# A padded identity, matmuls and one-row tables in place of DRAM round trips in a linear-attention and rational-FFN kernel

## The chip, the cores and the metric

The kernel runs on one core of a Trainium2 chip. The metric is the device time of one execution in microseconds. Three runs of the kernel before took 593.08, 595.28 and 597.16 us; their median is 595.28 us. All inputs and outputs are float32 in DRAM.

## The reference

Eight heads of size 48, a batch of 4 and 768 steps of a decayed linear attention, and then a feed-forward layer whose activation is a quotient of two polynomials:

```python
for t in range(S):
    cur = einsum('bhd,bhe->bhde', u * k[t], v[t])          # bonus of the present step
    y[t] = einsum('bhd,bhde->bhe', r[t], state + cur)
    state = w[..., None] * state + einsum('bhd,bhe->bhde', k[t], v[t])
h = x @ w_in                                               # x: y as 3072 x 384, w_in 384 x 2048
g = (a0 + a1*h + a2*h**2 + a3*h**3) / (1 + |b0|*|h| + |b1|*h**2 + 1e-6)
out = g @ w_out                                            # w_out 2048 x 384
```

The decay `w` and the bonus `u` are tables of 8 x 48 = 384 numbers.

## The kernel before

**Attention.** The 3072 tokens are 24 blocks of 128 (`blk`, L306: block n is batch n % 4). A block's k and r are scaled by powers of the decay (`scale_k`, `scale_r`), transposed on TensorE (`tk`, `tr`, L375), multiplied with each other (`a`, L398 and L399) and masked; k and v give the state's growth (`kv`, L420 and L421), and `y` (L448) joins both. The state that a block leaves is multiplied by the decay over a block, `w128` (`carry`, L459), for the block of the same batch four numbers later. The bonus of the present step is worked out beside it: `bonus_a` (L356), `bonus_b` (times the table `ub`, L361), `bonus_sum`, `bonus_v`, and `y_ev` (L453) adds it. `x` (L467) transposes the sum for the feed-forward part.

**Feed-forward.** It runs in 97 slices (L500): `f1` (L491, nine matmuls, two of them a slice but for the last two), ten element-wise operations on ScalarE and VectorE (`z`, `q`, `t`, `ln`, `ex`; `u3`, `hi`, `p`, `d`, `lo`), and `f2` (L495 to L497, six matmuls, two a slice). The weights come as 28 pieces, each loaded (`cl`, L235), split by a short chain (`c0`, L246, to `co`, L266) into two rounded parts, and kept.

**The tables.** `pro_load` to `pro_natural` make the powers of the decay. `pro_last` leaves the decay over a block as one column of 384 numbers in three columns of 128 (`wl`), `pro_wl` writes it to DRAM (`wld`, L179) and `pro_w128` reads it back with heads of 48 on partitions 0 and 64 (L183, L184). `pro_uw` reads `u` and `w` into all 128 partitions and `pro_ub` multiplies them on GpSimd (L150). `pro_squares` (L132 to L147, called `sq` below) works out constants of the quotient on VectorE. `pro_flag` (L198 to L211), `pro_flag_turn` and `pro_flag_min` test whether the inputs lie in the range of the fast formula; at the very end each engine loads the answer `okf` and branches over `general()` (L986, L987).

**What sets the order.** Every step is a task with engines, durations that the author wrote down, dependencies, buffers and a key. `run` (L783) plays them through a list scheduler: at each moment an engine takes the ready task with the lowest key whose buffers are free. The tasks are then issued in the order that came out, each engine's queue in that order. Where TensorE finds no ready task between 1.6 and 132.098 us of that play, a filler is put in its queue (L878 to L885, called warm): one matmul of 128 x 128 ones that nothing reads (L894). So a change of any task can move all others.

## Time and profile before

| what | us |
|---|---|
| median of three runs | 595.28 |
| the profiled execution: its own time | 593.54 |
| its span, first to last instruction | 591.8 |
| TensorE busy, of the span | 570.1 (96%) |
| VectorE busy | 506.0 (86%) |
| ScalarE busy | 454.6 (77%) |
| GpSimd busy | 179.7 (30%) |

The profile's page gives busy times by engine, and in the chain of waits the work that ended last at each moment. TensorE, 71% of that chain, is busy nearly all the time, but 739 of its 6194 matmuls are fillers, all of them before 138 us. The other engines do their table work, the splitting of the weights and the first half of the attention in that stretch. Later the span is the feed-forward part's two products, with the rest of the attention between them.

### The profile page before, as it was taken

How to read it: one execution, taken by the hardware profiler on the slowest of the kernel's cores; microseconds unless marked ns; L12 is line 12 of the kernel's file. 1: busy time of each engine (PE TensorE's matmuls, PEld its weight loads, DVE VectorE, ACT ScalarE, POOL GpSimd, SP SyncE). 2: the span in 40 equal slices, each digit the busy share in tenths (PEclk: the TensorE clock that was granted, in tenths of full speed). 3: DMA queues.
4: the chain of work that ended last, by engine and by line, in shares of the span. 5: the costliest groups of instructions: out<-in, count | busy, mean ns of one | idle time of the engine just before them, and what ended most of it. 6: DMA issues, size and time to landing. Idle time of an engine off the chain costs nothing.

```text
span 591.8 us, 15041 instructions
## 1 busy us (share of the span) xinstructions
PE 570.1 (96%) x6194; PEld 551.5 (93%) x6194; DVE 506.0 (86%) x791; ACT 454.6 (77%) x758; POOL 179.7 (30%) x199
## 2 busy tenths in 40 slices
PE   8969999999989999999999999999999999999996
PEld 7868998989989999999999988999999999999996
DVE  5669989899989889788899899788898897878784
ACT  8658678977968886888866857888778778778883
POOL 5677998996730000000240182000240100000000
PEclk9979999999989999999999999999999999999999
DMA  9886284964600000021221240020220000000000
GB/s 192 136 196 152 79 185 132 219 150 68 99 1 2 28 1 27 2 41 35 41 47 43 42 89 28 1 58 18 42 62 1 14 30 0 3 28 1 27 2 33
DMA packets 94269, 34.78 MB, mean 59 GB/s; under 512 B 87280, under 2 KB 90608, under 8 KB 94192
## 3 DMA queue, kind: packets, MB, share of 16 engines
q1 hardware_dynamic: 94192, 33.74, 26.4%
q8 instruction: 51, 0.84, 0.6%
q14 instruction: 26, 0.21, 0.1%
HBM read 29.01 MB, written 4.72 MB: 57 GB/s over the span
## 4 chain that ended last, share of the span: by engine, by line
PE 71%; DVE 11%; DMA 9%; ACT 5%; issue 2%; SPq 1%; POOL 0%; ACTq 0%; DVEq 0%
PE h L491 29%; PE o L495 10%; PE o L496 10%; PE o L497 10%; DMA sto<-in_moe_w_out_dram 4%; DMA sti<-in_moe_w_in_dram 3%; PE y L448 2%; PE kv L420 2%; PE a L398 1%; DMA kh<-in_k_dram 1%; DVE q L554 1%; PE warm L894 1%; ACT cp L246 1%; PE tk L375 1%; PE x L467 1%
## 5 line engine op out<-in xcount | busy, mean ns | idle before, releaser
L491 PE MATMUL h<-xthi,wi_hi 128*128 128x256 f32 x576 | 165.3, 287 | 1.9 <-DVE g L562 1.9
L491 PE MATMUL h<-xthi,wi_lo 128*128 128x256 f32 x576 | 163.2, 283 | 0.0
L491 PE MATMUL h<-xtlo,wi_hi 128*128 128x256 f32 x576 | 163.2, 283 | 0.0
L495 PE MATMUL o<-wo_hi,g 128*128 128x384 f32 x384 | 132.0, 344 | 0.0
L497 PE MATMUL o<-wo_hi,g 128*128 128x384 f32 x384 | 128.6, 335 | 0.0
L496 PE MATMUL o<-wo_lo,g 128*128 128x384 f32 x384 | 128.6, 335 | 0.0
L491 PEld LDWEIGHTS h<-xthi,wi_hi 128*128 128x128 f32 x576 | 110.0, 191 | 2.7 <-issue 2.2
L491 PEld LDWEIGHTS h<-xthi,wi_lo 128*128 128x128 f32 x576 | 110.4, 192 | 0.0
L491 PEld LDWEIGHTS h<-xtlo,wi_hi 128*128 128x128 f32 x576 | 110.3, 191 | 0.0
L522 ACT ACTIVATE q<-h 128x512 f32<-128x512 f32 (+1 forms) x97 | 57.5, 593 | 67.8 <-PE h L491 67.3
L550 DVE SCALAR_TENSOR_TENSOR g<-h,sig,z 128x512 fp32r<-128x512 f32 (+1 forms) x97 | 72.1, 744 | 38.5 <-ACT z L540 34.7
L526 ACT ACTIVATE q<-q,off,root 128x512 f32<-128x512 f32 (+1 forms) x97 | 78.4, 808 | 0.4
L531 ACT ACTIVATE t<-h,off,root 128x512 f32<-128x512 f32 (+1 forms) x97 | 74.6, 769 | 4.8 <-PE h L491 4.5
L554 DVE SCALAR_TENSOR_TENSOR q<-q,sig,g 128x512 f32<-128x512 f32 (+1 forms) x97 | 75.0, 774 | 2.5
L544 DVE SCALAR_TENSOR_TENSOR h<-t,sig,h 128x512 f32<-128x512 f32 (+1 forms) x97 | 72.1, 743 | 4.5 <-ACT q L522 2.5
L558 DVE SCALAR_TENSOR_TENSOR h<-h,sig,q 128x512 f32<-128x512 f32 (+1 forms) x97 | 72.8, 751 | 2.7
L536 ACT ACTIVATE z<-q,lnb 128x512 f32<-128x512 f32 (+1 forms) x97 | 69.9, 720 | 4.2 <-DVE g L562 2.0
L495 PEld LDWEIGHTS o<-wo_hi,g 128*128 128x128 f32 x384 | 72.4, 189 | 0.7
L496 PEld LDWEIGHTS o<-wo_lo,g 128*128 128x128 f32 x384 | 72.5, 189 | 0.0
L497 PEld LDWEIGHTS o<-wo_hi,g 128*128 128x128 f32 x384 | 72.1, 188 | 0.0
L540 ACT ACTIVATE z<-z,lnb 128x512 f32<-128x512 f32 (+1 forms) x97 | 69.7, 718 | 2.6
L562 DVE TENSOR_TENSOR g<-h,z 128x512 fp32r<-128x512 f32 (+1 forms) x97 | 65.9, 679 | 1.0
(129 smaller groups left out, 957.4 us busy)
## 6 DMA issues: line engine op xcount, KB each, us to landing
sti<-in_moe_w_in_dram SPq DMA_DIRECT2D x12, 512.0 KB, 5.6
sto<-in_moe_w_out_dram SPq DMA_DIRECT2D x16, 384.0 KB, 3.8
vn<-in_v_dram SPq DMA_DIRECT2D x24, 192.0 KB, 3.2
rh<-in_r_dram SPq DMA_DIRECT2D x24, 192.0 KB, 3.7
kh<-in_k_dram SPq DMA_DIRECT2D x24, 192.0 KB, 4.4
out_dram<-os SPq DMA_DIRECT2D x24, 192.0 KB, 1.9
vs<-in_v_dram SPq DMA_DIRECT2D x19, 96.0 KB, 4.1
ub<-in_u_dram SPq DMA_DIRECT2D x1, 192.0 KB, 4.3
```

Source lines behind the costliest of these rows:

```text
L491: nc.tensor.matmul(o, wt_[:, cc, ts(j, P)], x_[:, cc], start=(n == 0), stop=(n == 3 * NCC - 1))
L495: nc.tensor.matmul(o, hi, wo_hi[:, j], start=(j == 0), stop=False)
L496: nc.tensor.matmul(o, hi, wo_lo[:, j], start=False, stop=False)
L497: nc.tensor.matmul(o, lo, wo_hi[:, j], start=False, stop=(j == NJ - 1))
L526: nc.scalar.activation(g["q"], g["q"], AF.Square, scale=RB, bias=KB)
L531: nc.scalar.activation(g["t"], g["h"], AF.Square, scale=RA, bias=KA)
L536: nc.scalar.activation(g["z"], g["q"], AF.Ln, scale=2.0 ** -LN_SHIFT, bias=lnb[:, 2:3])
L540: nc.scalar.activation(g["z"], g["z"], AF.Exp, scale=-1.0, bias=lnb[:, 1:2])
L544: nc.vector.scalar_tensor_tensor(g["h"], g["t"], KAP, g["h"], op0=ALU.add, op1=ALU.mult)
L550: nc.vector.scalar_tensor_tensor(g["hi"], g["h"], c0, g["z"], op0=ALU.add, op1=ALU.mult)
L554: nc.vector.scalar_tensor_tensor(g["q"], g["q"], qe, g["hi"].bitcast(F32), op0=ALU.add, op1=ALU.mult)
L558: nc.vector.scalar_tensor_tensor(g["h"], g["h"], c0, g["q"], op0=ALU.add, op1=ALU.subtract)
```

## The change

The column `wl` is re-laid on TensorE: the identity is a slice of a wider zeroed tile `identw`, so that a shifted slice of it picks 48 of 128 rows and drops them at partition 0 or 64 (`pro_pairs`, ten matmuls into one PSUM tile; ScalarE copies it to `w128`). `u` and `w` are read into one partition, multiplied there, spread to all partitions by a matmul with a row of ones (`pro_spread`) and copied out by ScalarE (`pro_ub_all`, task `ube`). The range test's first part gets the key 400 and waits for slice 64 of 97.

```diff
--- before.py
+++ after.py
@@ -60,7 +60,9 @@
 
 
     wones = cst.tile([P, P], mybir.dt.bfloat16, name="wones")
-    ident = cst.tile([P, P], F32, name="ident")
+    identw = cst.tile([P, D + P + D], F32, name="identw")
+    ident = identw[:, D : D + P]
+    ones = cst.tile([1, P], F32, name="ones")
     mask = cst.tile([P, HALF], F32, name="mask")
     wraw = cst.tile([P, NCC], F32, name="wraw")
     wcol = cst.tile([P, NCC], F32, name="wcol")
@@ -73,7 +75,6 @@
     sq = cst.tile([P, NCC], F32, name="sq")
     cen = cst.tile([P, NCC], F32, name="cen")
     wl = cst.tile([P, NCC], F32, name="wl")
-    wld = dram.tile([DM], F32, name="wld")
     wrn = cst.tile([P, H, D], F32, name="wrn")
     wkn = cst.tile([P, H, D], F32, name="wkn")
     w128 = cst.tile([P, NP], F32, name="w128")
@@ -97,7 +98,9 @@
         nc.sync.dma_start(wraw, w.rearrange("h d -> (h d)").rearrange("(c p) -> p c", p=P))
         tab["zero"] = at.tile([P, P], F32, tag="m", name="zero", bufs=NM)
         nc.gpsimd.memset(tab["zero"], 0.0)
+        nc.gpsimd.memset(identw, 0.0)
         make_identity(nc, ident)
+        nc.vector.memset(ones, 1.0)
         nc.gpsimd.memset(wones, 1.0)
 
     def pro_mask():
@@ -113,9 +116,9 @@
         nc.sync.dma_start(coef[:, 4:6], b.partition_broadcast(P))
 
     def pro_uw():
-        nc.sync.dma_start(ub, u.partition_broadcast(P))
-        tab["wb"] = at.tile([P, H, D], F32, tag="m", name="wb", bufs=NM)
-        nc.sync.dma_start(tab["wb"], w.partition_broadcast(P))
+        for nm, src in (("ur", u), ("wr", w)):
+            tab[nm] = at.tile([1, H, D], F32, tag="m", name=nm, bufs=NM)
+            nc.sync.dma_start(tab[nm].rearrange("o h d -> o (h d)"), src.rearrange("h d -> (h d)").unsqueeze(0))
 
     def pro_beta():
         nc.scalar.activation(beta[:, 0:2], coef[:, 4:6], AF.Abs)
@@ -147,7 +150,15 @@
         v_.tensor_scalar(lnb[:, 2:3], QE, 2.0 ** -LN_SHIFT, None, op0=ALU.mult)
 
     def pro_ub():
-        nc.gpsimd.tensor_mul(ub, ub, tab.pop("wb"))
+        nc.gpsimd.tensor_mul(tab["ur"], tab["ur"], tab["wr"])
+
+
+    def pro_spread():
+        tab["up"] = ps_a.tile([P, 512], F32, tag="pa", name="pup")
+        nc.tensor.matmul(tab["up"][:, 0:DM], ones, tab["ur"].rearrange("o h d -> o (h d)"), start=True, stop=True)
+
+    def pro_ub_all():
+        nc.scalar.copy(ub.rearrange("p h d -> p (h d)"), tab["up"][:, 0:DM])
 
 
     def pro_clamp():
@@ -175,13 +186,20 @@
         nc.vector.tensor_mul(wl, tab["pw"][:, :, P], sq)
 
 
-    def pro_wl():
-        nc.sync.dma_start(wld.rearrange("(c p) -> p c", p=P), wl)
+    def pro_pairs():
+        p_ = tab["wp"] = ps_a.tile([P, 512], F32, tag="pa", name="pwp")
+        for h in range(H):
+            rows = slice(HALF * (h % 2), HALF * (h % 2) + D)
+            cs = range(h * D // P, (h * D + D - 1) // P + 1)
+            for c in cs:
+                x = D + h * D - c * P
+                nc.tensor.matmul(
+                    p_[rows, h // 2 : h // 2 + 1], identw[:, x : x + D], wl[:, c : c + 1], start=(c == cs[0]), stop=(c == cs[-1])
+                )
 
     def pro_w128():
-        wp = wld.rearrange("(p two d) -> two d p", two=2, d=D)
-        nc.sync.dma_start(w128[0:D, :], wp[0])
-        nc.sync.dma_start(w128[HALF : HALF + D, :], wp[1])
+        for rows in (slice(0, D), slice(HALF, HALF + D)):
+            nc.scalar.copy(w128[rows], tab["wp"][rows, 0:NP])
 
     def pro_turn(c, i):
         if c == 0:
@@ -672,7 +690,7 @@
             add(("sk", n), lambda e, n=n: scale_k(n, e), t, {"D": 0.47, "G": 0.96}, [("Lk", n), ("tab", 1)])
             add(("sr", n), lambda e, n=n: scale_r(n, e), t + 0.5, {"D": 0.47, "G": 0.96}, [("Lr", n), ("tab", 0)])
             add(("ba", n), lambda e, n=n: bonus_a(n, e), t + 2, {"G": 0.96, "D": 0.47}, [("sk", n), ("sr", n)], new=[("m", ("m", n))])
-            add(("bb", n), lambda e, n=n: bonus_b(n, e), t + 3, {"G": 0.96, "D": 0.47}, [("ba", n), ("ub",)], use=[("m", n)])
+            add(("bb", n), lambda e, n=n: bonus_b(n, e), t + 3, {"G": 0.96, "D": 0.47}, [("ba", n), ("ube",)], use=[("m", n)])
             add(("bs", n), lambda e, n=n: bonus_sum(n), t + 6, {"D": 0.47}, [("bb", n)], new=[("dt", ("dt", n))], use=[("m", n)])
             add(("bv", n), lambda e, n=n: bonus_v(n, e), t + 8, {"G": 0.96, "D": 0.47}, [("bs", n), ("Lv", n)], use=[("m", n), ("dt", n), ("v", n)])
             add(("tk", n), lambda e, n=n: trk_pe(n), t + 1, {"P": 0.44}, [("sk", n), ("id",), w_("a", n - 1)], new=[("ps", ("tk", n))])
@@ -744,6 +762,8 @@
         add(("beta",), lambda e: pro_beta(), 14, {"A": 0.8}, [("coef",)])
         add(("sq",), lambda e: pro_squares(), 16, {"D": 2.4}, [("beta",)])
         add(("ub",), lambda e: pro_ub(), 6, {"G": 0.96}, [("uw",)])
+        add(("ubp",), lambda e: pro_spread(), 6, {"P": 0.66}, [("ub",)], new=[("pa", ("up", 0))])
+        add(("ube",), lambda e: pro_ub_all(), 6, {"A": 0.37}, [("ubp",)], use=[("up", 0)])
         add(("cl_",), lambda e: pro_clamp(), -99, {"D": 0.13}, [("w",)])
         add(("ctr",), lambda e: pro_center(), -99, {"A": 0.55}, [("cl_",)])
         for c in range(NCC):
@@ -756,15 +776,15 @@
                 add(("turn", c, i), lambda e, c=c, i=i: pro_turn(c, i), -99 + c, {"P": 0.21},
                     [(("pow", "inv")[i], c), ("id",), first if c else None], new=[] if c else [("pa", new)], use=[new] if c else [])
             add(("tab", i), lambda e, i=i: pro_natural(i), -99, {"A": 0.37}, [("turn", c, i) for c in range(NCC)], use=[new])
-        add(("flag",), lambda e: pro_flag(), 200, {"D": 1.6}, [("cl_",), ("sq",)])
-        add(("flagt",), lambda e: pro_flag_turn(), 200, {"P": 0.1}, [("flag",)], new=[("ps", ("fl", 0))])
-        add(("flagm",), lambda e: pro_flag_min(), 200, {"D": 0.4}, [("flagt",)], use=[("fl", 0)])
+        add(("flag",), lambda e: pro_flag(), 400, {"D": 4.0}, [("cl_",), ("sq",), ("lo", 2 * NS // 3)])
+        add(("flagt",), lambda e: pro_flag_turn(), 400, {"P": 0.1}, [("flag",)], new=[("ps", ("fl", 0))])
+        add(("flagm",), lambda e: pro_flag_min(), 400, {"D": 0.4}, [("flagt",)], use=[("fl", 0)])
         add(("w",), lambda e: None, -99, {"S": 0.55})
         add(("wl",), lambda e: pro_last(), 10, {"D": 0.1}, [("pow", NCC - 1)])
-        add(("wld",), lambda e: pro_wl(), 10, {"S": 0.6}, [("wl",)])
-        add(("w128",), lambda e: pro_w128(), 12, {"S": 1.1}, [("wld",)])
-
-    COLS = {"turn": 256, "flagt": 256, "tk": 1024, "tr": 1024, "x": 768, "kv": 1180, "a": 1620, "y": 1736, "f1": 2304, "f2": 2304, "warm": 128}
+        add(("wp",), lambda e: pro_pairs(), 10, {"P": 0.6}, [("wl",), ("id",)], new=[("pa", ("wp", 0))])
+        add(("w128",), lambda e: pro_w128(), 12, {"A": 0.4}, [("wp",)], use=[("wp", 0)])
+
+    COLS = {"turn": 256, "flagt": 256, "tk": 1024, "tr": 1024, "x": 768, "wp": 40, "ubp": 1536, "kv": 1180, "a": 1620, "y": 1736, "f1": 2304, "f2": 2304, "warm": 128}
     TICK = 10.24 / 3
     ticks = {}
```

Because the order is worked out anew, the queues change around these steps. First SP's queue, the one that issues all transfers, at the place of the two table loads. Before (`ub`, `wb`: the two tables; `wld`, `w_94`: the round trip; `rh`, `kh`: r and k of a block; `sto`: a piece of w_out):

```order
L116 DMA ub<-in_u_dram 128x384
L118 DMA wb<-in_w_dram 128x384
L179 DMA wld<-wl 128x3x1
L322 DMA rh_113<-in_r_dram 128x8x48
L235 DMA sto_529<-in_moe_w_out_dram 128x768
L322 DMA rh_115<-in_r_dram 128x8x48
L112 DMA coef<-in_moe_a_dram 128x4
L113 DMA coef<-in_moe_b_dram 128x2
L235 DMA sto_593<-in_moe_w_out_dram 128x768
L183 DMA w_94<-wld 48x4x1
L184 DMA w_94<-wld 48x4x1
```

The same place now:

```order
L121 DMA ur<-in_u_dram 1x384
L121 DMA wr<-in_w_dram 1x384
L340 DMA rh_113<-in_r_dram 128x8x48
L340 DMA rh_115<-in_r_dram 128x8x48
L115 DMA coef<-in_moe_a_dram 128x4
L116 DMA coef<-in_moe_b_dram 128x2
L253 DMA sto_559<-in_moe_w_out_dram 128x768
L340 DMA kh_114<-in_k_dram 128x8x48
L340 DMA kh_116<-in_k_dram 128x8x48
L253 DMA sto_642<-in_moe_w_out_dram 128x768
```

The round trip's three transfers are gone, the tables are one row each, and the fifth and sixth weight pieces (`sto_559`, `sto_642`; before `sto_529`, `sto_593`) come behind both loads of `coef`, the sixth behind two loads of k as well.

Second, ScalarE's queue at the same time. Before (`cp<-sto`: the first step of splitting a piece, `c0`; `ysa<-tr`, `ysb<-tr`: the transposed r of block 3; `beta` to `root`: constants of `coef`):

```order
L246 ACTIVATE cp_595<-sto_529 128x384
L240 ACTIVATE upo_604<-sto_529 128x384
L269 COPY ysa_120<-tr_582 64x512
L269 CAST wo_hi<-bitso_565 128x384
L269 COPY ysb_121<-tr_582 64x512
L121 ACTIVATE beta<-coef 128x2
```

Now:

```order
L287 COPY ysa_120<-tr_579 64x512
L287 COPY ysb_121<-tr_579 64x512
L258 ACTIVATE upo_615<-sto_438 128x384
L287 CAST wi_hi<-bitsi_2_538 128x512
L264 ACTIVATE cp_644<-sto_559 128x384
L124 ACTIVATE beta<-coef 128x2
L125 ACTIVATE cabs<-coef 128x6
L128 ACTIVATE half<-rx 128x2
L129 ACTIVATE root<-half 128x2
L258 ACTIVATE upo_671<-sto_559 128x384
L287 CAST wo_hi<-bitso_692 128x384
L264 ACTIVATE cp_711<-sto_642 128x384
L161 COPY ub<-pup 128x384
```

The copies of block 3's transposed r, for which the product `a` of block 3 waits, now stand ahead of the fifth piece's first step, not behind it; the bonus table `ub` is written behind the first step of the sixth piece. On VectorE the fifteen operations of `sq`, which stood between the bonus of block 3 and its `y_ev`, now stand ahead of block 1's `bonus_b`, and so ahead of the whole bonus of blocks 0 and 1 and of the first `x`.

Third, VectorE and TensorE at the range test's end. Before, TensorE's transpose of the flag stood in the middle of the program:

```order
L375 MATMUL tr_4917<-ident,rh_115 128x128 x4
L375 MATMUL tr_4925<-ident,rh_111 128x128 x4
L215 MATMUL fl_4932<-ident,oks 1x128
L495 MATMUL o_0_4670<-wo_hi,g_4825 128x384
L496 MATMUL o_0_4670<-wo_lo,g_4825 128x384
```

Now it is TensorE's last instruction (`o_1_7856` is the output of the last token tile):

```order
L513 MATMUL o_1_7856<-wo_hi,g_8095 128x384
L514 MATMUL o_1_7856<-wo_lo,g_8095 128x384
L515 MATMUL o_1_7856<-wo_hi,g_8095 128x384
L233 MATMUL fl_8121<-identw,oks 1x128
L1006 TENSOR_LOAD okf
L1007 COMPARE_AND_BRANCH
```

The eleven VectorE operations of the test itself stand between `p` and `d` of slice 65; its result now passes TensorE and VectorE behind the last `f2`, and all engines load it after that.

TensorE's queue holds 896 fillers where it held 739. Ahead of the first `x` there are 295 (before 218): 44 of them between block 3's `a` and the spread of the bonus row, and 116 between the spread and that `x`, where 47 stood between `a` and `x` and 47 more ahead of `a` (25 there now). Between the first `x` and the last filler there are 601 (before 521).

## Rows read from the trace of the kernel before

**Rows 1.** Windows: length, busy PE, PEld, DVE, ACT, POOL, then TensorE clock, DMA share, GB/s.

```profile
20.00:40.00 20.00, 14.21 (x256) 13.30 (x254) 11.93 (x25) 8.84 (x21) 13.49 (x14) 0.83 0.81 125
...
60.00:80.00 20.00, 20.00 (x373) 18.97 (x368) 18.44 (x30) 13.26 (x26) 18.79 (x20) 1.00 0.31 82
...
200.00:250.00 50.00, 50.00 (x351) 49.90 (x351) 43.76 (x62) 39.03 (x60) 0.00 (x0) 1.00 0.03 12
```

**Rows 2.** Chain of waits, merged: start us, us, what; 0 to 200 us.

```profile
21.23 10.87 DMA sto<-in_moe_w_out_dram
...
40.30 0.33 PE x L467 x3
...
51.31 0.79 DVE half L134
...
173.04 2.15 PE h L491 x18
```

**Rows 3.** Windows of 2 us, columns as in rows 1.

```profile
20.00:22.00 2.00, 1.80 (x47) 1.52 (x46) 1.96 (x4) 1.96 (x5) 1.65 (x2) 1.00 0.77 218
...
24.00:26.00 2.00, 2.00 (x32) 1.92 (x29) 1.07 (x3) 1.10 (x2) 1.00 (x1) 1.00 0.92 24
```

**Rows 4.** Waits between 20 and 42 us: total, times, longest.

```profile
ACT cp L246 <- DMA sto<-in_moe_w_out_dram: 6.3, 1, 6.3
...
PE a L398 <- ACT ysa L269: 5.1, 1, 5.1
...
DVE rx L124 <- ACT cabs L122: 3.1, 1, 3.1
```

**Rows 5.** Timeline of SP's queue: start us, us, issue.

```profile
20.16 0.43 SPq L179 DMA_DIRECT2D wld<-wl  x1
...
22.28 3.46 SPq L112 DMA_DIRECT2D coef<-in_moe_a_dram  x1
```

**Rows 6.** Transfers by kind on the page: count, size, median us to landing.

```profile
sto<-in_moe_w_out_dram SPq DMA_DIRECT2D x16, 384.0 KB, 3.8
...
coef<-in_moe_a_dram SPq DMA_DIRECT2D x1, 2.0 KB, 11.5
```

**Rows 7.** Timeline of TensorE, 24 to 36.8 us.

```profile
25.40 0.61 PE L375 MATMUL tr<-ident,rh 128*128 128x128 f32 x4
25.84 2.79 PE L894 MATMUL warm<-wones 128*128 128x128 bf16 x47
```

**Rows 8.** Timeline of ScalarE, 8 to 10.3 us, with idle time before.

```profile
10.21 0.59 ACT L269 COPY ysa<-tr 64x512 f32<-64x512 f32 x1 [1.57 <-PE tr L375]
```

**Rows 9.** Timeline of TensorE, the last fillers.

```profile
136.96 0.56 PE L894 MATMUL o<-wones 128*128 128x128 bf16 x7
```

**Rows 10.** Instructions on tile half, near the end of sq: durations, first and last start.

```profile
L146 DVE TENSOR_SCALAR sig<-half x1: 147/147/147, 55.8 to 55.8; 128x1 f32<-128x1 f32 x1
```

**Rows 11.** Instructions on the range test's tile okw, columns as before.

```profile
L198 DVE TENSOR_TENSOR okw<-wraw,wcol x1: 346/346/346, 162.9 to 162.9; 128x3 f32<-128x3 f32 x1
...
L211 DVE TENSOR_REDUCE oks<-okw x1: 163/163/163, 166.5 to 166.5; 128x1 f32<-128x8 f32 x1
```

**Rows 12.** Windows of 5 to 20 us, columns as in rows 1.

```profile
160.00:170.00 10.00, 8.11 (x51) 7.82 (x50) 9.86 (x22) 7.49 (x12) 5.13 (x6) 0.91 0.18 24
```

**Rows 13.** Timeline of VectorE, lo of slice 66.

```profile
446.02 0.69 DVE L562 TENSOR_TENSOR g<-h,z 128x512 fp32r<-128x512 f32 x1
```

**Rows 14.** Timeline of TensorE, f2 of slice 66.

```profile
451.50 0.34 PE L495 MATMUL o<-wo_hi,g 128*128 128x384 f32 x1
```

**Rows 15.** Chain of waits at the end.

```profile
586.30 0.19 PE o L497
```

**Rows 16.** Timeline of SP's queue, the last two output transfers.

```profile
586.60 1.19 SPq L600 DMA_DIRECT2D out_dram<-os  x2
```

**Rows 17.** Instructions of line L987, the branch.

```profile
L987 PEldq COMPARE_BRANCH  x1: 3736/3736/3736, 585.3 to 585.3; - x1
```

**Rows 18.** Instructions that load okf.

```profile
L986 PEldq TENSOR_LOAD <-okf x1: 485/485/485, 584.7 to 584.7; - x1
```

## The prediction

> **What bounds the kernel now.** I read the stages first [rows 1]. From 200 to 250 us TensorE is busy for 50.00 of 50 us at full clock, and VectorE for 43.76: from there on the end is the sum of TensorE's instructions, which this change does not touch. So the result is decided by how much TensorE time is lost before. From 60 to 80 us TensorE is busy for 20.00 of 20 us as well, but with fillers among its work, while VectorE (18.44) and GpSimd (18.79) are nearly full. From 20 to 40 us everything is loose: TensorE 14.21 of 20 at a mean clock of 0.83, VectorE 11.93, ScalarE 8.84, although the DMA engines count as busy for 0.81 of it at only 125 GB/s.
>
> Next the chain of waits [rows 2]: its largest early piece is one transfer of a weight piece, 10.87 us from 21.23; transfers of its kind take 3.8 us in the median [rows 6]. The windows of 2 us show how [rows 3]: from 20 to 22 us the engines are busy for 0.77 and move 218 GB/s; from 24 to 26 us they are busy for 0.92 and move 24. I call this the crawl. It begins just after the round trip's write was issued at 20.16 and while the second table load was in the rings [rows 5]. Whatever was in flight came late: ScalarE waited 6.3 us for the piece, TensorE's product `a` of block 3 waited 5.1 us for a copy that stands behind it on ScalarE, and VectorE 3.1 us for `cabs`, which needs `coef` [rows 4].
>
> **The change, part by part.** The profiled execution took 593.54 us, its span 591.8; the median of the three runs is 595.28, 1.74 above it. I sum differences and put them on the median; on the profiled execution's own time the same sum holds.
>
> *Small new work.* Ten tiny matmuls and two small ScalarE copies for `w128` come while ScalarE sits idle for 1.57 us ahead of the first `ysa` copy [rows 8]: nothing. If that cover were gone, the copies would cost less than 0.6 us each, the price of the larger copy in that row. The spread has no row of its own kind. Bounds: 384 columns at the rate of `f1` (18 matmuls of 256 columns in 2.15 us [rows 2]) are 0.18 us; four times that, for full float32, is 0.72. I take 0.6, the upper side, as its operands are float32 and those of `f1` are not. It lies on TensorE's path to the first `x`.
>
> *The first `x`: from 40.3 to 38.3 us, -2.0.* Before, block 3's `tr` began at 25.40, 47 fillers followed to 28.63 [rows 7], and then `a` waited. Now its copies stand ahead of the fifth weight piece on ScalarE. From 25.4: `tr` 0.6, two copies of 0.59 [rows 8], `a` (estimated like one `f1`, 1.1) gives 28.3; 44 fillers at 59 ns (47 in 2.79 us [rows 7]) 2.6; the spread 0.6; 116 fillers 6.8: 38.3. VectorE must have `y_ev` of blocks 0 and 1 ready by then, with `sq` now ahead of it: if the fifth piece lands 3.8 us after an issue near 21.5, ScalarE reaches it behind the two copies and two more steps near 28.5, `beta` is done near 30, `sq` (51.3 to 56.0, 4.7 us [rows 2, 10]) near 35, and the six bonus steps of 384 columns, 0.52 us each by `lo`'s 0.69 for 512 [rows 13], end near 38.1. Both paths agree. Bounds: with the crawl as before, `coef` comes at 33.8 (11.5 us after 22.28 [rows 5, 6]), and the same chain ends near 42.6 (+2.3); without any filler in the way, near 31.5 (-8.8). I take -2.0, as the fillers do not go away.
>
> *Fillers behind the first `x`: +4.7.* 80 more of 59 ns. In rows 1 TensorE has no gaps from 60 to 80 us, so I count them in full; if they fall into waits, they cost nothing. The kernel's own work behind the first `x` is only reordered, so it sums to zero; the last filler stood at 137.5 us [rows 9].
>
> *`sq` leaves the crowded stretch: -4.0.* Its 4.7 us lay on the chain from 51.31 [rows 2], on an engine that is over 92% busy from 60 us on. Between 0 (TensorE's own queue sets the pace) and -4.7; nearer the latter, since the chain names it.
>
> *The range test leaves 163 to 167 us: -3.0.* Eleven operations from 162.9 to 166.7, 3.7 us [rows 11]. TensorE is busy for 8.11 of the 10 us around it, at a mean clock of 0.91 [rows 12]. Both losses together are about 2.8 us. Between 0 and -3.7.
>
> *The test at its new place: 0.* Near slice 65, `lo` of slice 66 ended at 446.71 and its `f2` began at 451.50 [rows 13, 14]: a cover of 4.8 us against 3.7 of work, with the rest of the attention beside it. If the cover is gone, up to +1.5. What is late next would be `lo`.
>
> *The end: +1.0.* The flag's transpose now stands behind TensorE's last `f2`, which ended at 586.49 [rows 15], with a reduction and a cast behind it and a load of 0.49 us [rows 18] on all engines. That puts the branch at about 588; TensorE's branch took 3.74 us [rows 17], to 591.7 or so. Before, the last output transfers, issued from 586.60 to 587.79 [rows 16], set the end, and most of this lies beside their landing. Between 0 and +3.
>
> Sum: -2.0 + 4.7 - 4.0 - 3.0 + 0 + 1.0 = -3.3 (the spread is inside the first term): 592.0 from the median, 590.2 for the profiled execution.
>
> **Two rules against rows.** Rows 3 and 5 show the crawl right behind the round trip's write. The Trainium skill's page DMA: Bandwidth & Descriptors, section Why small descriptors are slow (HBM only), prices small pieces by a fixed overhead, with 32 bytes of descriptor each; as an estimate from that page, 384 single numbers are 12 KB, 0.06 us at 218 GB/s. By that rule the write could not have held other transfers up for 6 us, and the crawl would have to come from something that stays: this is rival B. No row separates the two yet.
>
> Rows 17 show a branch of 3.74 us. The Trainium skill's page Runtime: NRT & Kernel Launch, section Instruction fetch mechanics, says that a taken branch to code outside the sequencer's window has to wait until that code is fetched. The trace agrees, and it speaks against a flag that is known only at the end: rival D.
>
> **Rivals.**
> A. *Fillers cost nothing.* They fall into waits that TensorE would have had. For: VectorE and GpSimd are nearly full from 60 to 80 us. Against: TensorE is, too. Time: 592.0 - 4.7 = 587.3.
> B. *The crawl stays*, because `coef` or plain load makes it. For: `coef` is still spread from one address to all partitions right there. Against: it starts with the parts that go. The first `x` at 42.6 in place of 38.3: 592.0 + 4.3 = 596.3.
> C. *Slower: TensorE's dense queue pays for a late start.* Place: from the first `x` to the last filler. If the queue sets the pace, nothing that VectorE gains arrives (`sq` 0, test 0), fillers cost 4.7 and the end 1.0, and every delay of the first `x` is added. It is slower by more than 1% once that `x` comes after 40.6 us (0.3 + 4.7 + 1.0 is 1% of 595.28). With the crawl's 42.6: 2.3 + 4.7 + 1.0 = +8.0, 603.3. For: 20.00 of 20 us, and `sq` ahead of the bonus. Against: the wait of 5.1 us is gone from the order whatever the transfers do.
> D. *The branches stand behind everything.* The end costs 3.0, the test's removal brings nothing: 592.0 + 2.0 + 3.0 = 597.0.
> That the change does not do what it says applies to the range test: its first part moves to the last third, its result to the very end. That is in the sum.
>
> **Chances and range.** The forecast 0.52 (its own range 588.5 to 596), A 0.15, B 0.15, C 0.10, D 0.08. A measurement of this kernel tells about 1%, 5.95 us, from no change. Faster by more: most of A, whose 587.3 lies 8.0 below, and a seventh of the forecast: 0.20. Slower by more: C and the far end of B and D: 0.11. Within 1%: 0.69. A range of 586.5 to 600 leaves out the lower part of A and nearly all of C, less than 0.2.
>
> **What would show it.** No window from 22 to 30 us with a high DMA share and under 60 GB/s; the fifth piece landed within 5 us; no wait of `a` of block 3; the first `x` at 37 to 39.5 us; the last filler between 132 and 139 us; no gap of TensorE at 160 to 170 us; `f2` of slice 66 not waiting; the last engine past its branch near 591 in the old count, about 5 us behind the last `f2`. Wrong would be a crawl without the round trip, a first `x` after 41 us, or a loss that grows after 200 us, where I count none.

## The result and the profile after

The changed kernel takes 598.80 us in the median of 18 runs (597.62 to 601.14), the kernel before 596.48 in 18 runs (593.08 to 600.30): a ratio of 1.0043 (95% interval 1.0024 to 1.0062). It was forecast at 592.0, 3.3 us faster than before; it is 2.3 us slower. Medians are over all runs; the ratios leave out the one slow run among them (603.57 us, u2_spread_only). The profiled executions differ by more, 591.8 to 597.1 us of span, because that of before (593.54 us) lies at the low end of its runs. The sums below are of these two executions, and so show a loss of 5.2 us where the medians show 2.3.

The windows of the changed kernel, with the columns of [rows 1], first the stages:

```profile
20.00:40.00 20.00, 16.56 (x274) 14.74 (x272) 19.17 (x30) 10.89 (x25) 15.72 (x15) 0.84 0.52 113
60.00:80.00 20.00, 19.31 (x350) 17.97 (x347) 19.75 (x28) 12.32 (x25) 17.05 (x16) 1.00 0.47 110
160.00:170.00 10.00, 10.00 (x80) 10.00 (x79) 9.73 (x16) 9.93 (x18) 0.00 (x0) 1.00 0.28 72
200.00:250.00 50.00, 50.00 (x354) 49.97 (x353) 44.36 (x63) 39.15 (x61) 0.00 (x0) 1.00 0.05 17
```

then those of 2 us that answer to [rows 3]:

```profile
22.00:24.00 2.00, 2.00 (x58) 1.88 (x53) 1.60 (x3) 1.94 (x4) 2.00 (x3) 1.00 0.56 60
24.00:26.00 2.00, 2.00 (x31) 1.98 (x30) 2.00 (x1) 0.91 (x3) 2.00 (x3) 1.00 1.01 272
26.00:28.00 2.00, 2.00 (x52) 1.90 (x49) 1.95 (x3) 1.95 (x4) 0.57 (x1) 1.00 1.19 212
```

The crawl, the stretch in which the transfers hardly moved, is gone (24 to 26 us: 272 GB/s, before 24), and so is the gap of [rows 12] (10.00 of 10 where there were 8.11). But VectorE, loose before between 20 and 40 us (11.93 of 20), is full there with 19.17. The waits between 20 and 46 us (total, times, longest) have a new first line for TensorE:

```profile
PEld pup L158 <- issue: 3.5, 1, 3.5
PE pup L158 <- issue: 3.3, 1, 3.3
POOL bitso L278 <- DVE bitso L273: 2.9, 1, 2.9
```

and TensorE's timeline (start, us, instruction, tiles, in brackets the idle time before it) shows what follows:

```profile
28.13 2.63 PE L914 MATMUL warm<-wones 128*128 128x128 bf16 x44
34.08 1.61 PE L158 MATMUL pup<-ur,ones 1*128 1x384 f32 x2 [3.33 <-issue]
35.63 8.93 PE L914 MATMUL warm<-wones 128*128 128x128 bf16 x116
45.44 0.52 PE L485 MATMUL x<-identw,m 128*128 128x128 f32 x3 [0.88 <-DVE m L471]
```

The spread (`pup`) waits 3.3 us, the granted clock is at half (0.50) from 34 to 40 us, the 116 fillers take 8.93 us, and the first `x` comes at 45.4. VectorE's timeline says why the wait of 0.88 us in front of `x` is on VectorE too:

```profile
23.06 4.06 DVE L284 TENSOR_TENSOR wi_lo<-bitsi,wi_hi 128x512 fp32r<-128x512 f32 x1 [0.40 <-ACT wi_hi L287]
...
33.42 0.55 DVE L273 SCALAR_TENSOR_TENSOR bitso<-sto,cp 128x384 int32<-128x384 int32 x1
...
34.50 0.15 DVE L136 RECIPROCAL half<-root 128x2 f32<-128x2 f32 x1
34.68 0.85 DVE L137 TENSOR_TENSOR half<-half,rx 128x2 f32<-128x2 f32 x1
35.56 0.94 DVE L138 TENSOR_TENSOR root<-root,half 128x2 f32<-128x2 f32 x1
36.53 0.93 DVE L139 TENSOR_SCALAR root<-root 128x2 f32<-128x2 f32 x1
...
42.35 0.15 DVE L150 TENSOR_SCALAR lnb<-sig 128x1 f32<-128x1 f32 x1
42.42 0.55 DVE L379 TENSOR_TENSOR m<-m,ub 128x384 f32<-128x384 f32 x1
```

`sq` takes 8.0 us, from 34.50 to 42.50, and the bonus begins behind it. Before, counted in the same way from its first step to its last, it took 5.1 (51.12 to 56.18; 4.7 in the prediction, which counts from its second step). Eight of its fifteen steps on one or two numbers a partition last 0.59 to 1.04 us, the others 0.13 to 0.17. GpSimd's timeline beside it:

```profile
22.92 0.99 POOL L153 TENSOR_TENSOR ur<-ur,wr 1x384 f32<-1x384 f32 x1
23.88 0.50 POOL L477 TENSOR_TENSOR vs<-vs,w 48x192 f32<-48x192 f32 x1
24.34 1.27 POOL L278 TENSOR_TENSOR bitsi<-bitsi,upi 128x512 int32<-128x512 int32 x1
25.57 0.99 POOL L374 TENSOR_TENSOR m<-rh,kh 128x384 f32<-128x384 f32 x1
...
34.52 0.99 POOL L278 TENSOR_TENSOR bitso<-bitso,upo 128x384 int32<-128x384 int32 x1
35.48 1.01 POOL L370 TENSOR_TENSOR rh<-rh,wrn 128x384 f32<-128x384 f32 x1
36.45 0.99 POOL L379 TENSOR_TENSOR m<-m,ub 128x384 f32<-128x384 f32 x1
```

Each of the eight long steps ends within 0.03 us of the end of a GpSimd operation; `wi_lo`, 0.69 to 1.40 us in its four other places on VectorE, lasts through four of them and ends 0.56 us behind the last. The kernel before has the same in its 5.1 us, in four of the fifteen steps. One of them, and the GpSimd operation that ends with it:

```profile
53.57 1.13 DVE L142 TENSOR_TENSOR off<-ctmp,half 128x2 f32<-128x2 f32 x1
53.42 1.26 POOL L260 TENSOR_TENSOR bitsi<-bitsi,upi 128x512 int32<-128x512 int32 x1
```

At the end the flag's transpose stands behind the last `f2`, as forecast, and TensorE's branch follows at 592.1 us:

```profile
590.22 0.34 PE L515 MATMUL o<-wo_hi,g 128*128 128x384 f32 x1
590.39 0.27 PE L233 MATMUL fl<-identw,oks 128*1 128x128 f32 x1
```

```profile
L1007 PEldq COMPARE_BRANCH  x1: 3378/3378/3378, 592.1 to 592.1; - x1
```

The span in four stretches, before and after: to the first `x` 40.1 and 45.4 us (+5.3); to the last filler 97.2 and 95.8 (-1.4); to `f1` of slice 90 417.4 and 417.5 (+0.1); to the end 37.1 and 38.3 (+1.2). By this account the loss is in the first.

### The profile page after: what moved, and what is told of

Same layout as the page of the kernel before. It is cut to its first block, busy times and chain, and to the rows that moved or that the text cites. A ratio compares the mean times of both kernels' runs of the same rounds, so it can differ in the third digit from the quotient of the medians.

```text
span 597.1 us, 15392 instructions
## 1 busy us (share of the span) xinstructions
PE 579.9 (97%) x6373; PEld 560.5 (94%) x6373; DVE 518.9 (87%) x798; ACT 455.9 (76%) x765; POOL 178.3 (30%) x192
## 4 chain that ended last, share of the span: by engine, by line
PE 78%; DVE 5%; POOL 2%; ACT 1%; DMA 1%; issue 1%; SPq 0%; DVEq 0%; POOLq 0%
PE h L509 32%; PE o L513 11%; PE o L515 10%; PE o L514 10%; PE o L914 3%; PE kv L438 3%; PE y L466 2%; PE a L416 2%; PE tk L393 1%; PE x L485 1%; PE tr L393 1%; DMA kh<-in_k_dram 1%; DVE ysa L427 1%; DVE vs L477 1%; DVE g L568 1%; DVE q L572 1%
## 5 line engine op out<-in xcount | busy, mean ns | idle before, releaser
L509 PEld LDWEIGHTS h<-xtlo,wi_hi 128*128 128x128 f32 x576 | 109.5, 190 | 0.0
## 6 DMA issues: line engine op xcount, KB each, us to landing
vn<-in_v_dram SPq DMA_DIRECT2D x24, 192.0 KB, 3.4
rh<-in_r_dram SPq DMA_DIRECT2D x24, 192.0 KB, 3.7
kh<-in_k_dram SPq DMA_DIRECT2D x24, 192.0 KB, 4.6
out_dram<-os SPq DMA_DIRECT2D x24, 192.0 KB, 1.9
```

Source lines behind the costliest of these rows:

```text
L509: nc.tensor.matmul(o, wt_[:, cc, ts(j, P)], x_[:, cc], start=(n == 0), stop=(n == 3 * NCC - 1))
```

## The experiments

All are read by the same moments of their profiled executions, and by the ratio to runs of the kernel before on the same chip:

| run | first `x` | last filler | `f1` of slice 18 | span | median | ratio (interval) |
|---|---|---|---|---|---|---|
| before | 40.1 | 137.3 | 185.2 | 591.8 | 596.5 | |
| changed | 45.4 | 141.2 | 191.5 | 597.1 | 598.8 | 1.004 (1.002 to 1.006) |
| e1_sq_late | 44.1 | 142.8 | 193.1 | 598.7 | 600.0 | 1.004 (1.001 to 1.007) |
| e2_bank | 44.9 | 142.1 | 192.5 | 598.1 | 600.4 | 1.008 (1.005 to 1.011) |
| e3_no116 | 45.4 | 143.5 | 193.9 | 599.2 | 600.8 | 1.006 (1.004 to 1.009) |
| e6_sq_bank | 41.9 | 140.9 | 191.1 | 596.2 | 598.3 | 1.003 (0.999 to 1.006) |
| e5_hold | 43.5 | 139.4 | 189.6 | 594.9 | 596.6 | one run |
| q1_plan_before | 35.3 | 133.1 | 180.5 | 587.3 | 588.5 | 0.986 (0.982 to 0.990) |
| u1_pairs_only | 36.4 | 133.8 | 180.3 | 587.1 | 586.5 | 0.982 (0.980 to 0.984) |
| u2_spread_only | 43.1 | 141.1 | 187.7 | 596.2 | 599.0 | 1.004 (1.001 to 1.007) |
| p1_flag_only | 43.1 | 141.2 | 185.4 | 595.2 | 596.1 | 0.999 (0.997 to 1.002) |
| q2_plan_flag | 35.2 | 131.6 | 176.8 | 587.0 | 588.4 | 0.987 (0.983 to 0.991) |
| t1_best | 35.2 | 132.1 | 176.4 | 585.2 | 587.8 | 0.985 (0.982 to 0.987) |
| s3_up_now | 33.6 | 143.1 | 188.3 | 595.3 | 598.3 | 1.003 (1.000 to 1.005) |
| w1_carry_back | 42.1 | 139.6 | 192.0 | 595.8 | 598.3 | 1.003 (0.999 to 1.006) |
| y1_less_fill | 45.5 | 142.6 | 195.6 | 600.8 | 600.6 | 1.006 (1.004 to 1.009) |
| w2_both | 42.7 | 140.7 | 192.4 | 596.7 | 598.7 | 1.004 (1.002 to 1.006) |
| v1_pairs_flag | 33.8 | 131.8 | 176.1 | 584.8 | 585.7 | 0.979 (0.975 to 0.984) |

**What delays the first `x`.** In the changed kernel, `sq` issued behind the first two `x`:

```diff
+        move(("sq",), ("xl", 1))
```

> The changed kernel, with the fifteen operations of sq issued on VectorE behind xl of block 1, not ahead of block 1's bonus_b; nothing else moved. Theory V (the first x came at 45.4 us because VectorE had sq, 7.9 us long, ahead of the bonus): the bonus steps end near 41 us, the first x is then set by the fillers and comes near 44.6, and what sq costs returns later; ratio to before 1.000 to 1.006. Theory B (the first x is late because the spread waited 3.3 us on TensorE and 116 fillers at half clock stand behind it): first x at 44.6 as well, but sq now lies in the crowded stretch: 1.004 to 1.010. Alone this run shows how long sq takes in another place.

The spread's output in a bank that nothing else has used yet:

```diff
-        tab["up"] = ps_a.tile([P, 512], F32, tag="pa", name="pup")
+        tab["up"] = ps_o.tile([P, 512], F32, tag="o0", name="pup")
```

> The changed kernel, with the spread's PSUM tile in a bank of its own (o0, unused until the first f2) in place of one of the two that the weight pieces use. Theory B: the wait of 3.3 us before the spread goes, TensorE stays at full clock, the first x comes near 38.5 to 40 us, ratio to before 0.990 to 0.996. Theory V: the spread comes near 31 us, but sq still ends near 42 and the first x stays at 44 to 45.4; ratio 1.002 to 1.005.

The 116 fillers between spread and first `x` left out:

```diff
+        order[a_:b_] = [x for x in order[a_:b_] if x[0][0] != "warm"]
```

> The changed kernel without the 116 filler matmuls between the spread and the first x. Theory F (fillers are what makes it slower): first x near 37, ratio 0.988 to 0.995. Theory V: the first x stays near 45, TensorE idles for some 9 us more and its clock stays at half until after it; ratio 1.003 to 1.010. Theory B: first x near 37, as under F.

And the first two edits together:

> Both edits at once: sq behind xl of block 1, and the spread in a bank of its own. If the two chains (V and B) are tied and each alone is hidden by the other, only this run moves the first x: to 38.5 to 40.5 us, ratio to before 0.992 to 0.998, less what sq gives back later. If it stays above 43 us, something else holds it.

TensorE's rows in e2_bank and then in e3_no116:

```profile
30.81 0.91 PE L158 MATMUL pup<-ur,ones 1*128 1x384 f32 x2
31.65 6.65 PE L914 MATMUL warm<-wones 128*128 128x128 bf16 x116
44.94 0.90 PE L485 MATMUL x<-identw,m 128*128 128x128 f32 x3 [6.64 <-DVE m L471]
```

```profile
34.08 0.88 PE L158 MATMUL pup<-ur,ones 1*128 1x384 f32 x2 [3.30 <-issue]
45.40 0.88 PE L485 MATMUL x<-identw,m 128*128 128x128 f32 x3 [10.45 <-DVE m L471]
```

With its own bank the spread waits for nothing and the fillers run at full clock (6.65 us for 8.93), yet `x` gains 0.5 us: it waits 6.64 us for VectorE. Without the fillers it gains nothing. So VectorE's chain held `x`, and the bank was second behind it; only both edits together bring 3.5 us, to 41.9, which is still later than the 38.5 to 40.5 expected: `x` there waits 3.7 us for VectorE, which had waited 2.8 us for GpSimd's part of the bonus. And none of the four is clearly faster at the end: with `sq` behind the first `x` the crowded stretch grows (98.7 us to the last filler, 95.8 in the changed kernel), and where TensorE waits instead of running fillers, the granted clock is 0.50 (36 to 46 us in e3_no116).

GpSimd made to wait until `sq` is done, by a small copy of its last result (`k_` is the place of `sq` in the list of tasks):

```diff
+        order.insert(k_ + 1, (("hold",), "G"))
```

> The changed kernel with one small GpSimd copy behind sq that waits for sq's last result, so that GpSimd work listed behind sq cannot run beside it. Theory V, its part on GpSimd (sq takes 8.0 us at 34.5 and 4.65 at 46 because GpSimd works beside it): sq takes about 5 us, from 34.5 to 39.5. Rival: sq's own latency for tiny operations that depend on each other is what it is, 7 to 8 us also with GpSimd quiet.

VectorE's rows there:

```profile
34.15 0.85 DVE L138 TENSOR_TENSOR half<-half,rx 128x2 f32<-128x2 f32 x1
35.04 0.16 DVE L139 TENSOR_TENSOR root<-root,half 128x2 f32<-128x2 f32 x1
35.23 0.17 DVE L140 TENSOR_SCALAR root<-root 128x2 f32<-128x2 f32 x1
```

GpSimd's last operation before its wait ends at 34.99; from then on the steps take 0.13 to 0.17 us, and `sq` 2.9 us instead of 8.0. The first `x` and the end both come about 2 us earlier in this one run, and not 5, since VectorE then waits 2.0 us for GpSimd's part of the bonus. This is shown: GpSimd's operations beside it stretch VectorE's.

**The code without the new order.** The planner got the old durations, engines and dependences, and the new code runs in the task order of before. Order here means also which engine takes a step, and the 739 fillers of before. The range test stays where it was, and the outputs of the pairs and of the spread lie in another bank:

```diff
-        add(("ub",), lambda e: pro_ub(), 6, {"G": 0.96}, [("uw",)])
-        add(("ubp",), lambda e: pro_spread(), 6, {"P": 0.66}, [("ub",)], new=[("pa", ("up", 0))])
-        add(("ube",), lambda e: pro_ub_all(), 6, {"A": 0.37}, [("ubp",)], use=[("up", 0)])
+        add(("ub",), lambda e: (pro_ub(), pro_spread(), pro_ub_all()), 6, {"G": 0.96}, [("uw",)])
...
+        add(("wld",), lambda e: (pro_pairs(), pro_w128()), 10, {"S": 0.6}, [("wl",)])
+        add(("w128",), lambda e: None, 12, {"S": 1.1}, [("wld",)])
```

> The matmuls for the pairs, the spread from one row and the two row loads in place of the round trip and the two table broadcasts, but in the task order of the kernel before (the planner is given the old durations, engines and dependences; both new matmul outputs lie in a bank of the output accumulators); range test unmoved. Theory Q (the new order, which the planner made from the new table, costs what the new code gains: VectorE works 197.7 us in the first 200 where it worked 186.8): without that order the crawl's 6 us come back, the first x at 33 to 36 us, the last filler at 131 to 134, span 586 to 588, ratio 0.991. Rival H (VectorE or the stream of weight pieces sets the pace to 140 us whenever the first x comes): first x as early, the last filler still at 136 to 138, span 591 to 592, ratio 1.000. If the crawl stays without round trip and broadcasts: first x at 40, span 592.

It is 1.4% faster than before and some 10 us faster than the changed kernel, with the same matmuls, copies and transfers in place of the round trip and the broadcasts:

```profile
27.11 0.91 PE L158 MATMUL pup<-ur,ones 1*128 1x384 f32 x2 [0.59 <-POOL ur L153]
...
35.29 0.50 PE L485 MATMUL x<-identw,m 128*128 128x128 f32 x3
```

The first `x` comes 10.2 us earlier than in the changed kernel, and the last filler, 97.9 us behind it, 8.1. Theory Q holds: the new order costs what the new code gains. The banks differ too: the spread's alone brought nothing in the new order (e2_bank), and the pairs', which run at 8.1 us in the changed kernel with nothing waiting for them, was not tried alone.

**Which part ends the crawl.** The same kernel with the old table loads, so that the pairs alone are new; and with the old round trip, so that the spread alone is:

```diff
-        for nm, src in (("ur", u), ("wr", w)):
...
+        nc.sync.dma_start(ub, u.partition_broadcast(P))
```

> The matmuls for the pairs alone in place of the DRAM round trip, in the task order of before; both tables still loaded to all partitions. If the round trip's write of single numbers makes the crawl (theory W): no window of 22 to 28 us under 60 GB/s, first x at 35 to 37, span 587 to 588, ratio 0.988. If the two table loads from one address make it (theory X): crawl as before (22 to 28 us at 24 to 60 GB/s), first x at 39 to 43, span 591 to 595, ratio 1.000.

```diff
-    def pro_pairs():
...
+    def pro_wl():
+        nc.sync.dma_start(wld.rearrange("(c p) -> p c", p=P), wl)
```

> The spread from one row alone, in the task order of before; the DRAM round trip stays. Theory W: crawl as before, first x at 39 to 43 us, span 591 to 595, ratio 1.000. Theory X: no crawl, first x at 35 to 37, span 587 to 588, ratio 0.988.

Windows of u1_pairs_only, then of u2_spread_only:

```profile
22.00:24.00 2.00, 2.00 (x72) 1.92 (x70) 0.84 (x2) 1.00 (x5) 0.42 (x1) 1.00 0.86 108
24.00:26.00 2.00, 1.19 (x35) 1.06 (x34) 1.53 (x3) 1.81 (x4) 1.98 (x2) 1.00 1.00 249
```

```profile
22.00:24.00 2.00, 2.00 (x66) 1.93 (x64) 0.50 (x2) 0.03 (x1) 1.89 (x2) 1.00 0.68 28
24.00:26.00 2.00, 0.16 (x6) 0.04 (x2) 0.00 (x0) 0.00 (x0) 1.80 (x2) 1.00 0.37 17
26.00:28.00 2.00, 0.00 (x0) 0.00 (x0) 0.00 (x0) 0.00 (x0) 0.00 (x0) 0.91 0.42 22
```

The round trip makes the crawl: without it no window of 20 to 28 us falls under 100 GB/s, although both broadcasts are loaded; with it alone the rings move 17 to 28 GB/s for 6 us. It is the write: the reads back are issued only at 31.3 us there, and at 29.9 in the kernel before, when the crawl is over or nearly so. What in the write makes it, the single numbers or the way to DRAM, was not tried. The pairs alone are worth 1.8%, the spread alone nothing or a little loss.

**The range test.** Moved alone, in the kernel before:

```diff
-        add(("flag",), lambda e: pro_flag(), 200, {"D": 1.6}, [("cl_",), ("sq",)])
+        add(("flag",), lambda e: pro_flag(), 400, {"D": 4.0}, [("cl_",), ("sq",), ("lo", 2 * NS // 3)])
```

> The kernel before with the move of the range test alone; the order of the work up to about 150 us is that of before. Theory N (the test's move gains what the prediction sized): the 3 us of TensorE time lost at 160 to 170 us come back, the end costs 1.2 us as in the changed kernel, so the span is 590.0 (591.8 - 3.0 + 1.2) and the ratio 0.997. Rival Z (the test's old place cost nothing net, the end costs 1.2): span 593.0, ratio 1.002.

With it, in the order of before, the whole change:

> The whole change (pairs, spread and moved range test) in the task order of before up to about 150 us. By Q and N together: span 584 to 586, ratio 0.988. By H and N: span 590, ratio 0.997. By H and Z: 593, 1.002.

And the same with the flag's transpose and minimum behind `f1` of slice 70, the transpose in one of the two common banks:

```diff
+        bank["fl", 0] = "pa"
+        move(("flagt",), ("f1", 70, 1))
+        move(("flagm",), ("flagt",))
```

> The whole change in the task order of before (as in the run q2_plan_flag), with the transpose and the minimum of the range test not behind the last products but behind f1 of slice 70, its flag thus known 130 us before the end. The end (from the last f2 to the last instruction: 5.33 us before, 6.50 in the changed kernel, 7.03 in q2_plan_flag) should be 5.3 to 5.5 again: span 585.3 to 585.6, ratio 0.985. Rival: the end is set by the last output transfers and the branch whatever the flag does: span 587.

The gap at 160 to 170 us closes in p1_flag_only (first row), and between `f1` of slices 12 and 16 it gains 3.3 us (q2_plan_flag 1.9 against q1_plan_before). But at 355 to 365 us a wait of TensorE for VectorE, 0.9 us long before and 1.3 now, is followed by a lower clock (second row; before 8.73 at clock 1.00), and 2.0 us are given back between `f1` of slices 50 and 60; q2_plan_flag shows the same, ten microseconds earlier:

```profile
160.00:170.00 10.00, 10.00 (x78) 10.00 (x77) 9.93 (x16) 9.81 (x17) 7.71 (x8) 1.00 0.47 99
355.00:365.00 10.00, 8.30 (x72) 7.80 (x71) 9.68 (x14) 4.63 (x8) 5.19 (x6) 0.83 0.12 41
```

The rest goes at the end, 6.7 us from the last `f2` to the last instruction in p1_flag_only and 7.0 in q2_plan_flag, where before has 5.3. With the early transpose it is 5.7. So with a late flag the move is worth about nothing, between theories N and Z: the medians of q1_plan_before and q2_plan_flag are 588.45 and 588.42. With an early one the span is 2.1 us shorter in one pair of executions (q1_plan_before and t1_best); their medians, 0.6 us apart with intervals that overlap, don't show it.

**What is wrong with the new order.** A bank that the planner needn't find for the spread, and the row product, spread and copy first by key:

```diff
-        tab["up"] = ps_a.tile([P, 512], F32, tag="pa", name="pup")
+        tab["up"] = ps_o.tile([P, 512], F32, tag="o0", name="pup")
...
-        add(("ubp",), lambda e: pro_spread(), 6, {"P": 0.66}, [("ub",)], new=[("pa", ("up", 0))])
+        add(("ubp",), lambda e: pro_spread(), -50, {"P": 0.66}, [("ub",)])
...
```

> The changed kernel, in which the planner needn't find a free PSUM bank for the spread (its output lies in a bank of the output accumulators, and the table no longer asks for one of the two common banks), and the row product, spread and copy come first by key. In the order that results, the spread stands directly behind the row product where 36 tasks of others stood between them, sq goes behind the first x by itself, and 186 fillers stand ahead of that x where there were 295. Theory K (what made the new order bad is the bank that the spread asks for: it put bonus, and with it the first x, behind VectorE and GpSimd work for later blocks): first x at 34 to 37 us, the last filler 95 to 98 us behind it, span 586 to 590, ratio 0.988. Rival L (the order behind the first x is as bad: more of the work is given to VectorE there): first x as early, the last filler no earlier than 138, span 593 or more, ratio 0.996 or more.

The first `x` came at 33.6 us, as theory K said, and the last filler at 143.1, as its rival did: 109.5 us behind it. From 50 to 60 us TensorE is busy for 5.27 of 10 (first row; second row, one step of `sq` on VectorE):

```profile
50.00:60.00 10.00, 5.27 (x102) 4.68 (x99) 9.70 (x19) 4.72 (x9) 6.82 (x8) 0.73 0.50 120
...
51.66 4.17 DVE L145 TENSOR_TENSOR off<-ctmp,half 128x2 f32<-128x2 f32 x1
```

That step lasts through five GpSimd operations; behind `sq` stands a `y_ev`, from 56.46 us, and TensorE's `kv` begins at 57.11, after a wait of 4.7 us.

So this order of the planner's is worse behind the first `x` too. In the nine runs with the changed kernel's order or one near it (the rows of the table from the changed kernel to e5_hold, and the three runs below) the last filler comes at 139.4 to 143.5 us, wherever the first `x` comes between 41.9 and 45.5, and here at 143.1 with `x` at 33.6. From 20 us to `f1` of slice 18, VectorE has 255 operations in the changed kernel and 254 in q1_plan_before, and is busy for 162.9 and 145.8 us. Against the tenth percentile of the same code line and shape over six runs, these operations are 24 to 26 us longer in the one and 10 to 12 in the other, depending on which six; nearly all of it is in operations that GpSimd ran beside, and of those without GpSimd beside them none is longer by over 0.2 us. Three runs ask whether that sets the pace. The carrying products on the engines of before:

```diff
+        order[:] = [(x, back.get(x[1:], e) if x[0] == "ca" else e) for x, e in order]
```

> The changed kernel with the products that carry the state (48x192, on VectorE or GpSimd by the planner) given to the engine that had them in the kernel before: 11 go back to GpSimd, 4 to VectorE. Theory S (VectorE sets the pace behind the first x, and what makes it late are operations that GpSimd's stretch): VectorE has 7 operations of 0.7 us fewer, the last filler comes 3 to 5 us earlier, at 136 to 138, span 592 to 594, ratio 0.997. Rival G (GpSimd, 84% busy there, is as late as VectorE): last filler at 141 or later, span 597 or more, ratio 1.004 or more.

80 of the fillers behind the first `x` left out (`w_` lists the places of all fillers behind it):

```diff
+        cut = {w_[i * len(w_) // 80] for i in range(80)}
+        order[:] = [x for i, x in enumerate(order) if i not in cut]
```

> The changed kernel with 80 of the 601 fillers between the first x and the last filler left out, evenly spread, so that their number is that of before; all else in the same order. Theory P, the prediction's own term (TensorE's queue is dense there, each filler costs its 59 ns): the last filler comes 4.7 us earlier, at 136.5 us, span 592.4, ratio 0.997. Rival A (they fall into waits, VectorE sets the pace): last filler at 140.5 to 141.5, span 596.5 to 597.5, ratio 1.004.

Both:

> The changed kernel with both edits at once: the carrying products on the engines of before and 80 fillers fewer behind the first x. Each alone left the end where it was or moved it back (f1 of slice 18 at 191.5 us in the changed kernel, 192.0 with the carries back, 195.6 with fewer fillers). Theory T (VectorE and TensorE with its fillers are both full in that stretch, so that one cannot give what the other takes): together f1 of slice 18 comes at 187 to 189 us, span 592 to 594, ratio 0.997. Rival C (fewer fillers cost clock wherever TensorE waits, whatever VectorE does): f1 of slice 18 at 192 or later, span 597 or more, ratio 1.004 or more.

None is clearly faster. In w1_carry_back VectorE is busy for 7.4 us less from 20 us up to `f1` of slice 18, which comes 0.5 us later. With fewer fillers TensorE's clock falls in two stretches of the profiled execution (y1_less_fill, 602.48 us, one of the slowest of its twelve; the changed kernel has 1.00 in both windows):

```profile
60.00:80.00 20.00, 18.04 (x302) 16.59 (x301) 18.75 (x26) 12.43 (x25) 16.18 (x15) 0.91 0.45 103
140.00:160.00 20.00, 18.21 (x232) 16.80 (x230) 18.94 (x29) 14.18 (x30) 17.02 (x17) 0.91 0.49 87
```

Theories S, P and T all fell. What sets the time of the last filler inside the new order stays open; that the order as a whole costs 10 us is shown by q1_plan_before.

**The best version.** Pairs and moved test with the early transpose, no spread, order of before:

> What the runs so far leave as the best: the matmuls for the pairs and the moved range test with its transpose behind f1 of slice 70, in the task order of before; the tables loaded to all partitions as before, no spread. From the run of the pairs alone (span 587.1) and the 2.1 us between the runs q1_plan_before and t1_best: span 585.0, ratio 0.979. Rival (the test's move gains nothing beside the pairs, as between q1_plan_before and q2_plan_flag): span 587, ratio 0.982.

It takes 585.67 us, 2.1% less than the kernel before (0.975 to 0.984), and beats both the kernel before and the changed one. That the moved test adds to the pairs is not shown: the interval overlaps that of u1_pairs_only, and the 2.3 us between the two profiled executions are there at the first `x` already (36.4 and 33.8).

## Why the prediction was wrong

The step that failed is the first term: "The first `x`: from 40.3 to 38.3 us, -2.0". It came at 45.4, +5.3. What it said of the crawl was right. The crawl is made by the round trip and goes with it, so its rule against rows is settled for the rows: u1_pairs_only and u2_spread_only differ by the round trip, and the small write did hold others up for 6 us. What failed is what stood in its place, the two paths to the first `x` and the order that they belong to:

- *`sq` ahead of the bonus, 4.7 us.* I saw the move and took the old duration, in which four steps were stretched already (the 0.79 us of `half` in [rows 2] is one). It took 8.0, since GpSimd was busy beside it all the time (2.9 with GpSimd held). And it began at 34.5, not near 30, where `beta` was done as forecast: VectorE's queue ahead of it was full. `rx` took 1.22 us there for 0.17, and one `wi_lo` 4.06 us.
- *The spread, 0.6 us, then 116 fillers, 6.8.* The spread waited 3.3 us. With another bank it doesn't wait (e2_bank), and VectorE's `bitso`, which reads the bank of a weight piece, ended 0.1 us ahead of it. It then took 1.61 us, and with the half clock from 34 to 40 us the fillers took 8.93. I had costed the matmul, not the bank it writes to. The lower bound, 31.5 us without fillers, forgot the other path: without them `x` came no earlier (e3_no116).
- *The order.* I summed the new order piece by piece as if it were neutral where no piece had a price. q2_plan_flag shows that the same change in the old order puts `x` at 35.2 and takes 588.4 us: the new order, with its engines and fillers, costs 10 us. Nothing in the sum stood for it. `sq` and the bank account for 3.5 of the 10 us at the first `x` (e6_sq_bank) and for 0.3 at the last filler; the rest stays open.

Part of the +5.3 is the execution of before. p1_flag_only, in the same order up to there, has its first `x` at 43.1 us, and the medians differ by 2.3.

The other terms:

- *Fillers behind the first `x`, +4.7.* Not found: 80 fewer gain nothing (y1_less_fill: median 1.75 us longer, ratio 1.006 against 1.004 with intervals that overlap; span of the profiled execution 3.7 us longer, with the clock at 0.91 in two stretches). A TensorE that is busy with fillers for 20.00 of 20 us is not full.
- *`sq` out of the crowded stretch, -4.0.* Not measured alone: put back there, it lengthens that stretch by 2.9 us, but `x` then starts the stretch 1.3 us sooner, and the last filler comes 1.6 later (e1_sq_late). The two terms were to give +0.7 from the first `x` to the last filler, and it was -1.4.
- *The range test, -3.0; at its new place 0; the end +1.0.* The second step that failed, by 3 us: from the last filler to `f1` of slice 90 the sum had -3.0, and the changed kernel has +0.1. Each was about right where it was looked for: 3.3 us gained between slices 12 and 16 in p1_flag_only, 19.56 us from `f1` of slice 66 to that of slice 70 both there and in the kernel before, the end +1.2 in the changed kernel. What the sum lacked are, in p1_flag_only, the 2.0 us given back at 355 us; what takes the gain in the changed kernel stays open.
- *Its marks.* No crawl, the fifth piece landed 4.0 us after its issue (21.96 to 25.92), no wait of `a` of block 3, no gap at 160 us: as forecast. The first `x` and the last filler (141.2, forecast 132 to 139): not.

Of the rivals, B fell (no crawl in the changed kernel). A was right that the fillers don't cost their 59 ns each, but its time of 587.3 rests on the same first `x`. D's time of 597.0 is near the result by luck: the end is only 1.2 us late. C is nearest in kind: it put a late first `x`, `sq` ahead of the bonus and a dense queue together, and its point of 40.6 us was passed. Its 603.3 took the crawl's 42.6 us for `x` and the fillers as a cost; with 45.4 and no fillers its sum is 5.3 + 1.0 = 6.3, against 5.2 between the two profiled executions. Its rule that a delay of the first `x` is added nearly holds in the order of before: from before to q1_plan_before `x` moves by -4.9 and the last filler by -4.2, to p1_flag_only by +2.9 and +3.9. In the new order it doesn't: from the changed kernel to e6_sq_bank they move by -3.5 and -0.3.

Up to 150 us p1_flag_only is the kernel before, yet its first `x` comes 2.9 us later, behind a longer crawl:

```profile
24.00:26.00 2.00, 1.69 (x27) 1.38 (x23) 1.94 (x4) 1.20 (x3) 0.97 (x1) 1.00 0.99 7
26.00:28.00 2.00, 1.64 (x26) 1.66 (x27) 0.90 (x2) 0.26 (x1) 0.00 (x0) 1.00 0.01 5
28.00:30.00 2.00, 1.61 (x29) 1.43 (x26) 0.00 (x0) 0.00 (x0) 0.00 (x0) 1.00 0.12 38
```

So the crawl differs from run to run, and the single trace from which I read it had a short one. That is part of why the pairs alone gain 10 us in the medians and 4.7 between the profiled executions.

## What to carry to other kernels

Where a planner sets the order, a change of code is two changes. Run the new code in the old order first: here it was worth -1.4% alone, the parts that pay -2.1%, and the order that the planner made for it gave all of that back. A price read beside one set of GpSimd operations doesn't hold beside another: `sq` took 2.9, 4.6, 5.1 and 8.0 us in these runs. And a matmul costs also the wait for the bank that it writes, 3.3 us for the spread.

## What the runs showed of the hardware

- *VectorE beside GpSimd.* In the changed kernel the seven steps of `sq` with two inputs, and one of the scalar steps, took 0.59 to 1.04 us beside GpSimd; with GpSimd held (e5_hold) they took 0.15 to 0.17, but for the first, during which GpSimd was still at work. The other seven, with one input, took 0.13 to 0.17 in both. Longest were `wi_lo`, 4.06 us through four operations of GpSimd that followed each other closely, and `off` in s3_up_now, 4.17 us through five. The Trainium skill's page SBUF — State Buffer, section SBUF: two separate sides, says that the two engines share one pair of ports under an exclusive lock, held for the whole instruction, against VectorE operations in a two-port mode or, where the GpSimd operation reads SBUF, with two SBUF inputs. The trace agrees on the two-input steps of `sq`, down to their ends; that one operation had to let four or five pass stands in these traces alone.
- *A small write to DRAM* (1.5 KB, single numbers) was followed by some 6 us in which all transfers together moved 17 to 28 GB/s (u2_spread_only, 22 to 28 us; in the kernel before 24 and 22 from 24 to 28 us, in p1_flag_only 5 to 38 from 24 to 30). The Trainium skill's page DMA: Bandwidth & Descriptors, section Why small descriptors are slow (HBM only), gives, as the estimate in the prediction, less than 0.1 us for it; the measurement decides.
- *Fillers and the clock.* The same 116 took 6.65 us behind a spread that didn't wait (57 ns each) and 8.93 behind one that had waited 3.3 us (77 ns). Behind that wait the clock was 0.50 from 34 to 40 us and 0.96 from 40 to 46 with them; without them it was 0.50 from 36 to 46 us (e3_no116).
